# Shifted due times, corrected planned durations and a second row buffer in a planned attention-plus-experts kernel

## The chip, the cores and the metric

The kernel runs on one core of one Trainium2 chip. The metric is the device time of one execution in microseconds (us), the median of several runs. A difference under 0.3% can't be told from no change here.

## The reference, cut to what matters

Three layers follow each other. Linear attention gives 2304 tokens of 512 values; a gated layer maps each token 512 to 1536 to 512; and a router sends each token to one of 8 experts, each 512 to 1024 to 512.

```python
def phi(x):                                  # attention, 32 heads of 576 x 64, 128 features
    h = einsum('bhsd,md->bhsm', x, omega) - sum(x * x) / 2
    return exp(h - max(h)) / sqrt(m)
kv, z = einsum('bhsm,bhsd->bhmd', phi(k), v), sum(phi(k), axis=2)
x = einsum('bhsm,bhmd->bhsd', phi(q), kv) / (einsum('bhsm,bhm->bhs', phi(q), z) + 1e-6)
xn = x / sqrt(mean(x * x) + 1e-6) * rms_g    # gated layer, 2304 x 512
x = silu(xn @ w_gate) * (xn @ w_val) @ w_out
logits = x @ w_gate2 + modality_bias[modality_id]
e = argmax(logits); gate = softmax(logits)[e]
out = gate * (maximum(x @ w1[e], 0) @ w2[e]) # each token by its own expert
```

## The kernel before, in words

The program is not written in the order in which it runs. The code calls `plan.op(engine, cost, want, fn, ...)` for some 3100 pieces of work, each one or a few instructions, and names the buffers that each reads and writes. `Plan.run` then plays the pieces through with the planned durations (`cost`) and fixed delays between engines (`LAG`). At each moment an engine that is free takes, among the pieces whose inputs are there and whose buffers have room, the one with the lowest due time `want`. A piece with several possible engines goes to the first that is free. What comes out is one fixed list of instructions for each engine, and each engine works its list strictly in order, waiting where an input isn't there. So a due time or a planned duration changes no instruction's work: it changes its place in a list, and for pieces with a choice the engine.

The work in order of time: attention features of 18 tiles of 128 tokens (project L511 to L513, minimum L521, exponentials L527, transposes L542), sums over k (L576) and products with them (L727), normalization and RMS scaling (L778 to L791, on GpSimd or VectorE). Two tiles make a chunk; `enter` transposes its tokens (L1015), `hidden` multiplies them with the gate and value weights (L1036, two pieces of 12 matmuls per block of 128 columns, 12 blocks), `project` multiplies with the output weights (L1094). There are 9 chunks. Numbers are carried in two parts, a rounded one and a remainder; the remainder is a subtraction by the helper at L287, on VectorE or GpSimd.

The weights of the gated layer come in as 64-bit floats and are converted on VectorE (L844, L851, L859), then scaled and split. The experts' weights are scaled, split and written back to DRAM (`matrix`, L937 to L994) meanwhile.

`result` takes a finished chunk's two tiles: transposes (L1133), router products (L1160), scores (L1180 to L1185), and writes the rows to DRAM. Its row buffer `r` comes from the area `x2T`, which holds one tile. After the last two tiles the slots of the experts are found on VectorE (`late_values` L1594, `experts` L1635, `late_indices` L1671). A slot is 128 tokens of one expert. Three early slots, all of one expert, are worked while the routing goes on. Then 17 late slots follow: `fetch` reads the slot's expert number and loads its weights in four parts of 1 MB (L1708, on SyncE) into a ring of three places, GpSimd gathers the tokens (L1748), PE transposes them (L1737) and works up pieces (L1771, 24 matmuls of 128 columns) and down pieces (L1800, 6 matmuls of 512 columns), four of each per slot. Up to 8 more slots stand behind branches on the number of slots in use (`rest_plan`).

```python
key = len(o.costs) > 1 and e == "dve" and not o.phase, o.want, o.n
if (best is None or key < least) and all(b.at or self.free(b) for b in o.takes):
    best, least = o, key
```

Of the kernel before, what the change touches and what calls it, by code (L numbers as in the profile page):

```python
# [9 lines left out]
F32 = mybir.dt.float32  # L10
# [12 lines left out]
P = 128  # L23
# [17 lines left out]


class Buf:

# [18 lines left out]
class Plan:  # L63
# [6 lines left out]
    def __init__(self, view, banks):  # L70
        self.ops, self.view, self.banks, self.live = [], view, banks, {}
        self.phase, self.users, self.before = 0, {}, {}

    def op(self, eng, cost, want, fn, reads=(), writes=(), fills=(), after=(), lag=None, holds=()):
# [72 lines left out]
    def run(self):  # L147
# [4 lines left out]
        def enter(o):  # L152
            for e in o.costs:
                idle[e].append(o)
            heapq.heappush(events, (o.ready, o.n, None))

        for o in self.ops:
            if not o.missing:
                enter(o)
# [52 lines left out]
def kernel(  # L212
# [14 lines left out]
    nc = tc.nc  # L227
# [6 lines left out]
    KD = DM // P  # L234
# [102 lines left out]
    for j in range(2):  # L337
        area("x01", (f"xh{j}", 2048, 1), (f"xl{j}", 2048, 1))
    areas["x2s"], areas["x2T"] = areas["raw"], areas["v1"]
    area("xs", ("xh", 1024, 2), ("xl", 1024, 2))  # L340
    area("om", ("om", 1024, 2))
# [132 lines left out]
    def features(u, want, banks, q_bank):  # L474
# [73 lines left out]
        if i < EXACT:  # L548
# [9 lines left out]
        plan.op(  # L558
            "dve", 0.6, want,
            lambda: nc.vector.scalar_tensor_tensor(  # L560
# [267 lines left out]
    def block(f):  # L828
# [3 lines left out]
        for t in range(3):  # L832
# [9 lines left out]
        plan.op(  # L842
            "dve", 1.3, want,
            lambda: nc.vector.tensor_scalar(  # L844
# [156 lines left out]
    class Chunk:  # L1001
# [5 lines left out]
        def enter(self, j, want, after=()):  # L1007

            x = x_t.pop(2 * self.c + j)
            pt = buf("t", [P, KD, P], F32)  # L1010

            def transposes():
                xf = x.tile.rearrange("p h d -> p (h d)")
                for kk in range(KD):
                    nc.tensor.transpose(pt[:, kk, :], xf[:, kk * P : (kk + 1) * P], ident)  # L1015

            r = slice(j * P, (j + 1) * P)
            h, lo = self.x
            plan.op("pe", 0.43, want, transposes, reads=[x], writes=[pt], holds=self.x, after=after)
            plan.op(  # L1020
                "act", 0.48, want, lambda: nc.scalar.copy(h[:, :, r], pt.tile),
                reads=[pt], fills=[h],
            )
            plan.op(
                "dve", 0.6, want, lambda: rest(nc.vector, lo[:, :, r], pt.tile, h[:, :, r]),
                reads=[pt, h], fills=[lo],
            )
# [80 lines left out]
        def result(self, j, want, out_want):  # L1108
# [3 lines left out]
            plan.op(  # L1112
                {"act": 0.5, "dve": 0.6}, None, want,
                lambda e: copy_on(e, x2[:, :DM], self.acc[j].tile, 2.0),
# [3 lines left out]
            s2 = buf("s2", [P, 3], F32)  # L1118
            r = buf("x2T", [P, KD, P], F32)
            plan.op(  # L1120
# [10 lines left out]
            def transposes():  # L1131
# [14 lines left out]
            plan.op(  # L1146
                "dve", 0.6, out_want, lambda: rest(nc.vector, r.tile, pt.tile, top.tile),
                reads=[pt, top], writes=[r],
# [539 lines left out]
    def slots(plan, which, start, main):  # L1688
# [9 lines left out]
        def load(s, want):  # L1698
# [4 lines left out]
            def fetch(c, w):  # L1703
                if c == 0:
                    src_e = e0_i[0:1, 0:1] if s == 0 else slot_i[0:1, s : s + 1]
                    regs["e"] = nc.values_load(src_e, engines=(SP,), min_val=0, max_val=E - 1)
                src = split_dram[bass.ds(regs["e"], 1), c].rearrange("a p n -> p (a n)")
                nc.sync.dma_start(out=w.tile, in_=src)  # L1708
# [143 lines left out]
    while s < NSLOT:  # L1852
        group = range(s, min(s + (1 if s == NFIXED else 2), NSLOT))
        with tc.If(n_slots > s):
            rest_plan = Plan(view, banks)
            rest_plan.phase = 1
            for b in (idx, slot_i, sc_s, split_b, *x2_b):
                b.writers, b.readers = [], []
            slots(rest_plan, group, 0, False)
            rest_plan.run()  # L1860
# [71 lines left out]
```

## Time and profile before

| | us |
|---|---|
| runs, median (all) | 886.61 (884.8, 886.61, 887.37) |
| the profiled execution | 884.56 |
| its span, first to last instruction | 882.8 |
| PE busy | 832.1 |
| VectorE busy | 556.4 |
| ScalarE busy | 472.3 |
| GpSimd busy | 298.3 |

PE is TensorE's matmuls, PEld its weight loads, DVE VectorE, ACT ScalarE, POOL GpSimd, SP SyncE. A line number names a line of the kernel before, printed above. PEclk is the granted clock of TensorE as a share of 2.4 GHz; 0.5 is the lower level, 1.2 GHz. A busy share is a mean over stages with different limits, so the stages are to be read one by one.

### The profile page before, as it was taken

The numbers are of one execution on the slowest core, as the hardware profiler recorded it, in microseconds if no ns is written. First come the engines' busy times: TensorE is split into PE (matmuls) and PEld (weight loads), VectorE is DVE, ScalarE is ACT, GpSimd is POOL, SyncE is SP. The second block draws the span as 40 slices with busy tenths as digits, with TensorE's granted clock in tenths as the row PEclk, the third lists the DMA queues.
The fourth block names the chain that finished last, engine by engine and source line by source line (L and its number), as shares of the span: only waits on it lengthen the run. The fifth ranks groups of instructions, "written<-read, shape, count | busy, mean of one in ns | idle before, by whom it ended". The sixth has DMA issues, their size and how long they took to land. (4 is left out here: it accounts for less than half of the span.)

```text
span 882.8 us, 19258 instructions
## 1 busy us (share of the span) xinstructions
PE 832.1 (94%) x7482; PEld 690.6 (78%) x7482; DVE 556.4 (63%) x1284; ACT 472.3 (53%) x1114; POOL 298.3 (34%) x400
## 2 busy tenths in 40 slices
PE   7889999889999999999899999999997999999991
PEld 6778878678988888888788888888874777777770
DVE  6999699867768879868877979726472121121210
ACT  4764454476767778777767768432322333332230
POOL 0383468624324433424423423312312122122110
PEclk9979999899999999999999999999998999999997
DMA  8624353315376565574556664203319999999960
GB/s 289 220 102 175 120 185 126 144 60 169 119 251 216 185 226 201 171 294 156 198 191 215 223 237 181 108 1 149 104 50 384 424 425 424 424 424 424 425 280 12
DMA packets 39157, 192.29 MB, mean 218 GB/s; under 512 B 5135, under 2 KB 5263, under 8 KB 21648
## 3 DMA queue, kind: packets, MB, share of 16 engines
q1 hardware_dynamic: 35856, 180.92, 54.3%
q0 software_dynamic: 3200, 10.01, 2.9%
q8 instruction: 66, 1.08, 0.5%
q14 instruction: 35, 0.29, 0.1%
HBM read 147.88 MB, written 43.55 MB: 217 GB/s over the span
## 5 line engine op out<-in xcount | busy, mean ns | idle before, releaser
L1036 PE MATMUL bank<-x,big 128*128 128x256 f16 x2592 | 307.4, 273 | 3.8 <-DVE plain L1069 3.8
L1036 PEld LDWEIGHTS <-big 128*128 128x128 f16 x2592 | 246.8, 99 | 45.8 <-issue 17.5
L1094 PE MATMUL bank<-wo,hs 128*128 128x512 f32 x648 | 179.9, 414 | 1.2 <-POOL hs L287 1.2
L1094 PEld LDWEIGHTS bank<-wo,hs 128*128 128x128 f32 x648 | 116.4, 193 | 22.8 <-POOL hs L287 2.4
L287 POOL TENSOR_TENSOR hs<-plain,hs 128x256 fp32r<-128x256 f32 x92 | 76.9, 837 | 153.2 <-ACT hs L277 98.5
L1771 PEld LDWEIGHTS <-big 128*128 128x128 f16 x1920 | 112.3, 98 | 16.4 <-DMA big<-split_dram 1.6
L1771 PE MATMUL bank<-plain,big 128*128 128x128 f16 x1920 | 117.8, 219 | 2.6 <-DMA big<-split_dram 1.4
L1800 PE MATMUL bank<-big,plain 128*128 128x512 f16 x480 | 116.8, 382 | 0.7 <-DVE plain L287 0.7
L287 DVE TENSOR_TENSOR plain<-plain 128x512 f16<-128x512 f32 (+1 forms) x44 | 31.6, 720 | 127.5 <-ACT plain L277 127.3
L812 DVE SCALAR_TENSOR_TENSOR big<-big,e_fac 128x512 f16<-128x512 f32 x128 | 107.2, 860 | 6.2 <-ACT big L818 6.0
L1054 ACT ACTIVATE plain<-bank,w_scale 128x256 f32<-128x256 f32 x108 | 51.3, 475 | 84.6 <-PE bank L1036 65.4
L527 ACT ACTIVATE plain<-bank,plain 128x128 f32<-128x128 f32 x256 | 72.7, 370 | 24.7 <-DVE plain L521 21.4
L946 ACT ACTIVATE plain<-big,plain 128x1024 bf16<-128x1024 f32 x64 | 73.5, 1149 | 9.7 <-DMA big<-in_w_exp_dram 9.5
L1800 PEld LDWEIGHTS <-plain 128*128 128x128 f16 x480 | 44.6, 98 | 41.7 <-DVE plain L287 1.5
L818 ACT ACTIVATE big<-big,e_fac 128x512 f16<-128x512 f32 x103 | 72.0, 722 | 1.2 <-DMA split_dram<-big 1.2
L1061 DVE SCALAR_TENSOR_TENSOR plain<-plain,bank 128x256 f32<-128x256 f32 x108 | 44.4, 413 | 33.4 <-ACT plain L1054 33.0
L287 POOL TENSOR_TENSOR xs<-plain,xs 128x256 fp32r<-128x256 f32 x45 | 38.6, 860 | 71.3 <-ACT xs L277 55.6
L1788 ACT ACTIVATE plain<-bank 128x512 f32<-128x512 f32 x40 | 23.9, 598 | 68.8 <-PE bank L1771 68.5
L521 DVE TENSOR_REDUCE plain<-bank 128x4 f32<-128x512 f32 x66 | 45.1, 683 | 16.7 <-PE bank L513 12.4
L1069 DVE SCALAR_TENSOR_TENSOR plain<-bank,w_scale,plain 128x256 f32<-128x256 f32 x108 | 51.1, 477 | 0.6
L277 ACT CAST hs<-plain 128x256 fp32r<-128x256 f32 x84 | 33.8, 405 | 30.8 <-DVE plain L1069 21.7
L1815 POOL TENSOR_TENSOR plain<-plain,x 128x1 f32<-128x1 f32 x17 | 3.9, 231 | 130.7 <-ACT plain L818 100.8
(252 smaller groups left out, 1186.2 us busy)
## 6 DMA issues: line engine op xcount, KB each, us to landing
big<-split_dram SPq DMA_DIRECT2D x72, 1024.0 KB, 21.6
big<-in_w_exp_dram SPq DMA_DIRECT2D x32, 1024.0 KB, 6.8
split_dram<-big SPq DMA_DIRECT2D x32, 1024.0 KB, 8.6
big<-in_w_moe_dram SPq DMA_DIRECT2D x36, 512.0 KB, 4.5
plain<-in_v_dram SPq DMA_DIRECT2D x18, 260.0 KB, 3.9
x_dram<-plain SPq DMA_DIRECT2D x18, 258.0 KB, 3.5
plain<-in_kT_dram SPq DMA_DIRECT2D x16, 256.0 KB, 2.9
plain<-in_qT_dram SPq DMA_DIRECT2D x16, 256.0 KB, 2.7
```

The lines of the kernel that those rows point to most:

```text
L287: eng.tensor_tensor(out=out, in0=src, in1=hi, op=ALU.subtract)
L521: lambda: nc.vector.tensor_reduce(out=mx.tile, in_=pp.tile, axis=AX.X, op=ALU.min),
L527: nc.scalar.activation(ph[:, h, :], pp[:, h, :], AF.Exp, bias=mx[:, h : h + 1], scale=-1.0)
L812: nc.vector.scalar_tensor_tensor(out=out, in0=src, scalar=factor, in1=hi, op0=ALU.mult, op1=ALU.subtract)
L818: nc.scalar.activation(out, src, AF.Copy, scale=factor)
L946: lambda c=c, h=h, cs=cs: nc.scalar.activation(junk.tile, raws[c][:, cs], AF.Square, bias=tiny, accum_out=sums[:, 2 * c + h : 2 * c + h + ...
L1036: nc.tensor.matmul(gv[:, t, :], w[a][:, kk, :], self.x[x][:, kk, :], start=kk == 0 and m == 0, stop=kk == KD - 1 and m == 2,)
L1054: lambda: nc.scalar.activation(th.tile, gv[:, 0, :], AF.Tanh, scale=w_scale[:, f, 2:3]),
L1069: lambda: nc.vector.scalar_tensor_tensor(out=th.tile, in0=gv[:, 1, :], scalar=w_scale[:, f, 4:5], in1=th.tile, op0=ALU.mult, op1=ALU.mult,),
L1094: nc.tensor.matmul(self.acc[j].tile, a[:, r], w_in(f, i, 2), start=f == 0 and m == 0, stop=f == FT - 1 and m == 2,)
L1771: nc.tensor.matmul(ph[:, j, :], w_of(c, p, k * F2 + (4 * n + j) * P, P), x[a][:, kk, :], start=kk == 0 and j == 0 and m == 0, stop=kk == K ...
L1800: nc.tensor.matmul(y.tile, hs[n][a][:, kk, :], w_of(2 + n, p, kk * DM, DM), start=f == 0 and m == 0, stop=f == KF2 - 1 and m == 2,)
```

## The change

A table `NUDGES` shifts the due times of 32 runs of pieces, by their number in the order of the calls, by -6 to +6; a due time of 12 more is one chunk, or one slot, later. The shifts are applied in `Plan.run` of the main plan alone, not in those behind the branches. Planned durations of some pieces on VectorE and ScalarE are set anew (0.6 to 0.68 or 0.69, 0.48 to 0.58, 0.5 to 0.6, 1.3 to 1.05). The last chunk's two tiles take their row buffer from an area of two places. Since a shift moves the third part of one slot's weights ahead of its first, `fetch` reads the expert number with whichever part comes first. No instruction is added or taken away in what is computed. Of the table one line and its end are shown.

```diff
--- before.py
+++ after.py
@@ -40,6 +40,18 @@
 EXPERTS_FROM, EXPERTS_TO = 25.0, 85.0
 
 
+
+NUDGES = (
+    (214, 214, 0.5), (257, 257, -2), (270, 270, 4), (288, 293, 1), (305, 311, -0.5),
...
+    (2549, 2549, -4), (3005, 3005, -2),
+)
+
+
 class Buf:
 
 
@@ -70,6 +82,7 @@
     def __init__(self, view, banks):
         self.ops, self.view, self.banks, self.live = [], view, banks, {}
         self.phase, self.users, self.before = 0, {}, {}
+        self.nudged = True
 
     def op(self, eng, cost, want, fn, reads=(), writes=(), fills=(), after=(), lag=None, holds=()):
 
@@ -154,6 +167,9 @@
                 idle[e].append(o)
             heapq.heappush(events, (o.ready, o.n, None))
 
+        for first, last, shift in NUDGES if self.nudged else ():
+            for o in self.ops[first : last + 1]:
+                o.want += shift
         for o in self.ops:
             if not o.missing:
                 enter(o)
@@ -337,6 +353,7 @@
     for j in range(2):
         area("x01", (f"xh{j}", 2048, 1), (f"xl{j}", 2048, 1))
     areas["x2s"], areas["x2T"] = areas["raw"], areas["v1"]
+    areas["x2E"] = areas["v1"] + areas["v0"]
     area("xs", ("xh", 1024, 2), ("xl", 1024, 2))
     area("om", ("om", 1024, 2))
     area("hs", ("hh", 1024, 2), ("hl", 1024, 2))
@@ -556,7 +573,7 @@
             reads=[pt], writes=[ft],
         )
         plan.op(
-            "dve", 0.6, want,
+            "dve", 0.68, want,
             lambda: nc.vector.scalar_tensor_tensor(
                 out=ft[:, 1], in0=pt.tile, scalar=PSC, in1=ft[:, 0],
                 op0=ALU.mult, op1=ALU.subtract,
@@ -840,7 +857,7 @@
             )
         lo32, hi32 = (lambda: raw[:, :, :, 0]), (lambda: raw[:, :, :, 1])
         plan.op(
-            "dve", 1.3, want,
+            "dve", 1.05, want,
             lambda: nc.vector.tensor_scalar(
                 bits.tile, hi32(), 3, 0x3FFFFFFF, ALU.logical_shift_left, ALU.bitwise_and
             ),
@@ -1018,11 +1035,11 @@
             h, lo = self.x
             plan.op("pe", 0.43, want, transposes, reads=[x], writes=[pt], holds=self.x, after=after)
             plan.op(
-                "act", 0.48, want, lambda: nc.scalar.copy(h[:, :, r], pt.tile),
+                "act", 0.58, want, lambda: nc.scalar.copy(h[:, :, r], pt.tile),
                 reads=[pt], fills=[h],
             )
             plan.op(
-                "dve", 0.6, want, lambda: rest(nc.vector, lo[:, :, r], pt.tile, h[:, :, r]),
+                "dve", 0.69, want, lambda: rest(nc.vector, lo[:, :, r], pt.tile, h[:, :, r]),
                 reads=[pt, h], fills=[lo],
             )
 
@@ -1110,13 +1127,13 @@
             i = 2 * self.c + j
             x2 = buf("x2s", [P, XC], F32)
             plan.op(
-                {"act": 0.5, "dve": 0.6}, None, want,
+                {"act": 0.6, "dve": 0.69}, None, want,
                 lambda e: copy_on(e, x2[:, :DM], self.acc[j].tile, 2.0),
                 reads=[self.acc[j]], writes=[x2],
             )
 
             s2 = buf("s2", [P, 3], F32)
-            r = buf("x2T", [P, KD, P], F32)
+            r = buf("x2E" if self.c == NCH - 1 else "x2T", [P, KD, P], F32)
             plan.op(
                 "act", 0.82, out_want,
                 lambda: nc.scalar.activation(
@@ -1144,7 +1161,7 @@
                 reads=[pt], writes=[top],
             )
             plan.op(
-                "dve", 0.6, out_want, lambda: rest(nc.vector, r.tile, pt.tile, top.tile),
+                "dve", 0.69, out_want, lambda: rest(nc.vector, r.tile, pt.tile, top.tile),
                 reads=[pt, top], writes=[r],
             )
             plan.op(
@@ -1701,7 +1718,7 @@
             regs = {}
 
             def fetch(c, w):
-                if c == 0:
+                if not regs:
                     src_e = e0_i[0:1, 0:1] if s == 0 else slot_i[0:1, s : s + 1]
                     regs["e"] = nc.values_load(src_e, engines=(SP,), min_val=0, max_val=E - 1)
                 src = split_dram[bass.ds(regs["e"], 1), c].rearrange("a p n -> p (a n)")
@@ -1853,7 +1870,7 @@
         group = range(s, min(s + (1 if s == NFIXED else 2), NSLOT))
         with tc.If(n_slots > s):
             rest_plan = Plan(view, banks)
-            rest_plan.phase = 1
+            rest_plan.phase, rest_plan.nudged = 1, False
             for b in (idx, slot_i, sc_s, split_b, *x2_b):
                 b.writers, b.readers = [], []
             slots(rest_plan, group, 0, False)
```

The first 52 pieces of PE keep their order; from there on the lists of all engines differ. Pieces with a choice of engine change it too: 33 pass from VectorE or ScalarE to GpSimd and 29 leave it. Three places follow. Lines of the changed kernel are 16 or 17 higher than those of the kernel before.

GpSimd, near 60 us, before: L779 to L791 is the RMS scaling of one tile (twice here), L287 a remainder, `xs` an attention input.

```order
L790 TENSOR_SCALAR plain<-plain 128x512
L791 TENSOR_TENSOR plain<-plain 128x512
L287 TENSOR_TENSOR xs<-plain,xs 128x256
L779 TENSOR_SCALAR plain<-plain 128x1
L780 TENSOR_TENSOR plain<-plain 128x1
L790 TENSOR_SCALAR plain<-plain 128x512
L791 TENSOR_TENSOR plain<-plain 128x512
L287 TENSOR_TENSOR wo<-big,wo 128x512
```

The same place of the changed kernel (L796 to L808 the scaling, L303 a remainder):

```order
L807 TENSOR_SCALAR plain<-plain 128x512
L808 TENSOR_TENSOR plain<-plain 128x512
L303 TENSOR_TENSOR xs<-plain,xs 128x256
L796 TENSOR_SCALAR plain<-plain 128x1
L797 TENSOR_TENSOR plain<-plain 128x1
L303 TENSOR_TENSOR xs<-plain,xs 128x256
L807 TENSOR_SCALAR plain<-plain 128x512
L808 TENSOR_TENSOR plain<-plain 128x512
L303 TENSOR_TENSOR wo<-big,wo 128x512
```

A second remainder of an attention input (`xs`) stands between the two halves of the second tile's scaling.

PE, near 435 us, before: L1160 is the end of a tile's router products, L1015 the transposes of a tile that enters a chunk, L1094 a projection; `bank_90` and the like are PSUM banks.

```order
L1160 MATMUL bank_90<-route_w,plain 128x16
L1160 LDWEIGHTS plain
L1160 MATMUL bank_90<-route_w,plain 128x8
L1015 MATMUL bank_90<-ident,plain 128x128 x4
L1094 MATMUL bank_93<-wo,hs 128x512 x3
L1094 MATMUL bank_94<-wo,hs 128x512 x3
```

The same transposes in the changed kernel (L1032; L744 products with the sums over k, L1111 a projection, L1053 gate or value products):

```order
L744 LDWEIGHTS plain
L744 MATMUL bank_91<-plain 64x65
L1111 MATMUL bank_93<-wo,hs 128x512 x3
L1111 MATMUL bank_94<-wo,hs 128x512 x3
L1032 MATMUL bank_92<-ident,plain 128x128 x4
L1053 LDWEIGHTS big
L1053 MATMUL bank_90<-x_393,big 128x256
```

The router products no longer stand ahead of the transposes, which write another bank than before.

VectorE, at the end of the routing, before: L1599 to L1606 end `late_values`, L1635 to L1644 begin `experts`.

```order
L1599 TENSOR_TENSOR x_393<-x_393,xs 128x504
L1605 TENSOR_SCALAR x_393<-x_393,xs 128x18x28
L1606 TENSOR_TENSOR x_393<-x_393,xs 128x18x28
L1635 TENSOR_SCALAR x_393<-x_393 128x1
L1636 TENSOR_SCALAR x_393<-xs,x_393 128x28
L1637 TENSOR_TENSOR x_393<-x_393 128x224
L1644 TENSOR_REDUCE x_393<-x_393 128x28
```

And in the changed kernel:

```order
L1616 TENSOR_TENSOR x_393<-x_393,xs 128x504
L1622 TENSOR_SCALAR x_393<-x_393,xs 128x18x28
L1623 TENSOR_TENSOR x_393<-x_393,xs 128x18x28
L303 TENSOR_TENSOR plain<-plain 128x512
L1652 TENSOR_SCALAR x_393<-x_393 128x1
L1653 TENSOR_SCALAR x_393<-xs,x_393 128x28
L1654 TENSOR_TENSOR x_393<-x_393 128x224
```

A remainder of an early slot's rows (L303) now stands between the two.

## Rows read from the trace of the kernel before

**Rows 1.** The page: busy time and share, then what the DMA queues moved by slice
```profile
PE 832.1 (94%) x7482; PEld 690.6 (78%) x7482; DVE 556.4 (63%) x1284; ACT 472.3 (53%) x1114; POOL 298.3 (34%) x400
...
GB/s 289 220 102 175 120 185 126 144 60 169 119 251 216 185 226 201 171 294 156 198 191 215 223 237 181 108 1 149 104 50 384 424 425 424 424 424 424 425 280 12
```

**Rows 2.** Windows by stage: length, busy (count) of PE, PEld, DVE, ACT, POOL; PEclk, DMA, GB/s
```profile
0.00:44.00 44.00, 36.79 (x232) 32.73 (x232) 34.43 (x72) 27.70 (x90) 9.41 (x19) 1.00 0.74 256
44.00:210.00 166.00, 154.12 (x1169) 132.01 (x1170) 142.45 (x252) 91.45 (x233) 93.49 (x106) 0.93 0.35 123
210.00:640.00 430.00, 425.11 (x3685) 368.23 (x3684) 323.70 (x837) 283.93 (x675) 152.18 (x219) 1.00 0.52 184
640.00:677.00 37.00, 29.99 (x304) 20.04 (x303) 20.20 (x74) 9.21 (x19) 5.65 (x8) 0.91 0.45 180
677.00:865.00 188.00, 186.14 (x2101) 137.62 (x2098) 35.61 (x53) 59.48 (x98) 36.55 (x47) 1.00 0.95 397
```

**Rows 3.** Windows, same columns: the stretches at the lower clock up to 640 us
```profile
43.70:53.90 10.20, 8.91 (x41) 8.51 (x42) 8.97 (x14) 4.65 (x11) 8.96 (x9) 0.50 0.07 27
64.20:67.60 3.40, 3.40 (x11) 2.11 (x9) 3.40 (x5) 2.87 (x9) 3.22 (x6) 0.50 0.76 251
166.60:173.40 6.80, 5.88 (x17) 4.40 (x16) 6.20 (x10) 3.85 (x11) 4.50 (x8) 0.50 0.66 254
197.30:200.70 3.40, 3.40 (x17) 2.67 (x17) 2.73 (x5) 0.38 (x1) 3.32 (x4) 0.50 0.00 0
436.20:439.70 3.50, 3.50 (x30) 2.51 (x29) 3.18 (x10) 2.63 (x9) 0.78 (x1) 0.51 0.89 227
```

**Rows 4.** Waits of PE: total us, times, longest us
```profile
PE bank L727 <- ACT plain L277: 2.9, 1, 2.9
...
PE bank L1015 <- POOL plain L791: 1.5, 1, 1.5
```

**Rows 5.** Timeline of POOL near 60 us: start, duration, engine, line, operation
```profile
61.12 1.26 POOL L791 TENSOR_TENSOR plain<-plain 128x512 f32<-128x512 f32 x1
```

**Rows 6.** Line L287 on POOL, input remainders: ns min/median/max, first and last start
```profile
L287 POOL TENSOR_TENSOR xs<-plain,xs x45: 717/732/2310, 45.9 to 525.8; 128x256 fp32r<-128x256 f32 x45
```

**Rows 7.** Timeline of DVE and PE, 432 to 436 us; idle before and releaser in brackets
```profile
432.61 0.44 PE L1160 MATMUL bank<-route_w,plain 128*128 128x24 bf16 x12
...
435.23 0.17 DVE L1180 TENSOR_REDUCE logits<-bank 128x8 f32<-128x24 f32 x1
...
435.55 0.63 PE L1015 MATMUL bank<-ident,plain 128*128 128x128 f32 x4 [2.49 <-DVE logits L1180]
```

**Rows 8.** Timeline of PE, 648 to 677 us
```profile
649.45 0.45 PE L1160 MATMUL bank<-route_w,plain 128*128 128x24 bf16 x12
...
652.78 0.17 PE L1447 MATMUL bank<-xs 128*128 128x8 bf16 x1
...
671.61 1.11 PE L1737 MATMUL bank<-ident,plain 128*128 128x128 f32 x4 [5.32 <-DMA plain<-x_dram,x]
...
676.85 0.33 PE L1771 MATMUL bank<-plain,big 128*128 128x128 f16 x3
```

**Rows 9.** Timeline of SyncE: the first loads of the late experts' weights
```profile
662.13 4.88 SPq L1708 DMA_DIRECT2D big<-split_dram  x8
```

**Rows 10.** Line L1708, the load issued at 792.0 us, and its landing
```profile
L1708 SPq DMA_DIRECT2D big<-split_dram x1: 333/333/333, 792.0 to 792.0; - x1
...
DMA to landing us min/median/max: 22.2/22.2/22.2
```

**Rows 11.** Line L1708, the load issued at 827.5 us, and its landing
```profile
L1708 SPq DMA_DIRECT2D big<-split_dram x1: 337/337/337, 827.5 to 827.5; - x1
...
DMA to landing us min/median/max: 19.2/19.2/19.2
```

**Rows 12.** Timeline of PE near 814 us
```profile
814.25 2.85 PE L1771 MATMUL bank<-plain,big 128*128 128x128 f16 x48 [1.45 <-DMA big<-split_dram]
```

**Rows 13.** Timeline of PE, its last products
```profile
859.37 5.34 PE L1800 MATMUL bank<-big,plain 128*128 128x512 f16 x24
```

5 rows, old and new, of the table NUDGES are left out of this document.

## The prediction

> **What bounds the kernel now.** I read the page first: TensorE is busy 832.1 of 882.8 us [rows 1], so what a change of order can give is its idle time and the work that it does at half clock. The windows by stage say where these lie [rows 2]. PE is idle for 44.0 - 36.8 = 7.2 us in the first 44 us, 166.0 - 154.1 = 11.9 from 44 to 210, 4.9 in the long stretch to 640, 7.0 in the routing (640 to 677) and 1.9 in the late experts; then 17.8 us of ending follow in which PE does nothing. DVE is busy 142 of 166 us between 44 and 210: there the weights of the gated layer are converted beside the attention, and PE waits for it and for POOL.
>
> Idle time costs twice where the granted clock falls. Rows 3 show five stretches at half of full clock (1.2 in place of 2.4 GHz) before 640 us. A piece of matmuls there takes about twice as long, so half of PE's busy time in them is lost: 8.9 / 2 = 4.5, then 1.7, 2.9, 1.7 and 1.75 us. The first begins within the longest wait before them [rows 4], the last with the wait of 2.5 us at 435 us [rows 7].
>
> The last 190 us have another limit. From 677 to 865 us the DMA engines are 95% busy, and their rate stays at 424 to 425 GB/s over seven slices of the page and 384 in the first [rows 1, 2]. The loads of the late experts' weights start at 662.1 us, when SyncE can read the experts' numbers [rows 9]. The part issued at 792.0 takes 22.2 us and lands at 814.2 [rows 10], and PE, after 1.45 us of waiting for it, begins at 814.25 [rows 12]. So PE's work before 814 doesn't set the end. Call S the time of the first load. The end of PE is S + (814.25 - 662.13 = 152.1) + the work that remains after that part, 50.5 us (PE's last products end at 859.37 + 5.34 = 864.7 [rows 13]): S + 202.6. What counts is when S comes and how much work stands behind each part.
>
> **The change part by part.** It adds and removes no computation, so I sum waits.
>
> First 44 us, and the wait of 2.9 us after it: PE's first 52 pieces keep their order, and ACT and DVE keep theirs in what feeds them, but for one 0.4 us piece on DVE. I take 0, and the 4.5 us of slow clock stay too.
>
> 44 to 210 us, the rest: 11.9 - 2.95 = 8.9 us of waits and 1.7 + 2.9 + 1.7 = 6.3 us of clock, 15.3 together. The new lists move the weights' pieces ahead of attention pieces by up to ten places on DVE, and attention pieces back by 10 to 20 places on PE. In the second half of this stretch a piece of attention and its successor stood four to nine pieces apart and now mostly seven to eleven, so that more work covers the same chain. Against it stands one place that gets worse. Near 60 us PE waited 1.5 us for the second half of an RMS scaling on POOL [rows 4], which starts its last instruction at 61.12 [rows 5]. Now a remainder of an input stands ahead of it, 0.73 us by the median and 2.31 at most [rows 6]; the wait becomes 2.2 to 3.8 us. Whether the rest closes half or all of its gaps no row shows. By the rows the ends are a gain of 15.3 and, if as many new waits open as old ones close and that one grows, a loss of 2.3. I take a gain of 6, somewhat under the middle, since ten waits are moved and some will reappear.
>
> The Trainium skill, "SBUF — State Buffer", section "Who interferes with whom", says that GpSimd and VectorE share one port pair, that a two-input VectorE instruction contends with GpSimd's reads, and that the one that comes first holds the pair. The spread from 717 to 2310 ns for one form [rows 6] agrees. By that rule the inserted remainder, which runs beside VectorE's weight pieces, costs the upper end, 2.3 us, where the median would say 0.7.
>
> 210 to 640 us: 4.9 us of waits and 1.75 of clock. At 435 us the transposes of a tile wait for the scores that read the same PSUM bank: the router products begin at 432.6, the first reading of the bank only at 435.2, behind other work on DVE, and PE stands for 2.49 us [rows 7]. The new order has the router products behind the transposes and another bank under these. 2.5 + 1.75 = 4.2 us go. What is late next there is the gate product behind it, which needs only DVE's usual pieces. The other 2.4 us are four short waits; I keep them and add 0.7 for new ones: a gain of 3.5. Ends: 6.6 gained, 2 lost (the same wait somewhere else).
>
> Routing, to S: ahead of the last router products [rows 8] two up pieces of 1.34 us now stand behind and one token transposition of 0.44 ahead: 2.2 us earlier. Three up pieces (4.0 us) stand between them and the rank products in place of 652.78 - 649.45 = 3.3: 0.7 later, and one remainder of 0.69 is put before the expert numbers on DVE: together 1.4 later. S comes 0.8 earlier. The second row buffer frees the last tile's square on ACT, but its transposes still stand behind the other tile's router products on PE, so I count it as nothing; at most it gives the 0.7 us of that square.
>
> The wait of 5.3 us for the gathered tokens at 671.6 [rows 8] shrinks, since two down pieces now go ahead of those transposes. I count nothing: the late experts follow the loads, and PE would only wait later.
>
> Late experts: behind the part that bound at 814 three pieces fewer remain. The new limit is the first part of the last slot. It is issued at 827.5 and lands 19.2 us later, at 846.7 [rows 11], or S + 184.6. In the new list 13 pieces follow from its first use, where 9 did, each 5.34 / 4 = 1.335 us [rows 13]: S + 201.9, against S + 202.6. A gain of 0.7. The moved load of one part delays two others of that slot by one part each; by the same count they end near S + 201, below that limit.
>
> Sum: 6 + 3.5 + 0.8 + 0.7 = 11.0 us. From the profiled execution's 884.56 (span 882.8 and 1.8 around it) this gives 873.6. The median of the runs is 2.05 higher, so I forecast 886.6 - 11.0 = 875.6 us.
>
> **The rivals.**
> - *The gaps only move.* The planner's fixed delays don't know a POOL instruction of 0.7 or 2.3 us [rows 6], so new waits open where it sees none. For it: 33 pieces go to POOL. Against: the 435 us place, where the cause itself is gone. Stage gains fall to 1 or 2 us: 885, within 0.3%.
> - *The place near 60 us turns the sign.* If the grown wait reaches 3.8 us, PE is at half clock again for as long as after the first wait, 10.2 us, where it was 3.4 [rows 3]: 2.3 for the wait and (10.2 - 3.4) / 2 = 3.4 for the clock, 5.7 us. Nothing behind takes it up, since S follows PE. It decides from the point where the remainder runs at 2.3 us; if the other gains before 640 us fail as well, only routing and late experts are left against it: 5.7 - 1.5 = 4.2 us slower, 890.8.
> - *All gaps close.* 15.3 + 6.6 + 1.5 = 23.4 us: 863.
> - *PE bounds the late experts after all.* If the loads run faster once they start, the 5.3 us at 671, and 1.7 for two short waits and as much for the clock before it, come off the end too: 6 to 8 us more, 868. Against: the flat 424 GB/s [rows 1]. The Trainium skill, "DMA: Bandwidth & Descriptors", section "Where 436 GB/s comes from", gives 435 GB/s as the ceiling, 2.5% above the trace; by an estimate from it 192 us of loads could shrink by 5 us at most.
>
> **How the numbers follow.** Chances: my forecast (869 to 882) 0.44, gaps only move 0.18, the sign turns 0.14, all gaps close 0.12, PE bounds the late experts 0.12. A difference under 0.3% (2.7 us) can't be told from none. Faster: 0.44 + 0.12 + 0.12 and a small part of the second case, 0.70. Same: 0.16. Slower: 0.14. The likeliest case's own range is 869 to 882; the one for 8 in 10 reaches over the gaps that only move and to the fuller gains: 863 to 888.
>
> **What would show it.** Right: a PE wait of about 2.9 us near 45 us as before; no wait of over 1 us at the transposes near 430 us; PE idle from 44 to 210 down to 6 us or so, with fewer stretches at 0.5; the first late load near 650 us; 201 to 203 us from it to PE's last product, with waits for the weights spread over the late slots in place of the one at the gather. Wrong: an interval from first load to end that is shorter than 198 us (then PE bounded that stage), a first load later than 662 us (then the gaps only moved), or a wait of over 3 us near 62 us with a long stretch at half clock.

## The result, and the profile after

The changed kernel takes 877.91 us (median of 4 runs, 875.57 to 879.51); the kernel before 886.12 (4 runs). The ratio is 0.991, 95% interval 0.989 to 0.9929: 8.2 us less, where 11.0 were forecast. The profiled execution of the changed kernel took 879.51, the highest of its four, and that of before 884.56, under its median; between these two traces there are 5.05 us.

The page of the changed kernel, the rows that answer to [rows 1]:

```profile
PE 830.9 (95%) x7482; PEld 691.3 (79%) x7482; DVE 564.5 (64%) x1286; ACT 467.3 (53%) x1108; POOL 307.7 (35%) x404
...
GB/s 291 221 118 160 193 103 127 156 61 113 194 248 217 217 210 209 198 239 131 208 237 154 219 220 203 145 19 227 22 118 416 426 425 424 424 425 424 424 177 24
```

The windows by stage, with the columns of [rows 2], and the stretches at half clock up to 640 us, as in [rows 3]:

```profile
0.00:44.00 44.00, 37.19 (x232) 33.01 (x232) 34.40 (x72) 27.99 (x90) 8.08 (x19) 1.00 0.74 256
44.00:210.00 166.00, 155.17 (x1191) 134.11 (x1192) 141.27 (x248) 94.34 (x245) 102.42 (x114) 0.95 0.35 123
210.00:640.00 430.00, 429.55 (x3782) 371.06 (x3780) 338.75 (x863) 280.85 (x671) 155.30 (x219) 1.00 0.53 185
640.00:677.00 37.00, 26.27 (x287) 19.64 (x285) 16.91 (x57) 7.24 (x13) 6.61 (x9) 0.89 0.70 280
677.00:865.00 188.00, 182.75 (x1999) 133.46 (x1997) 33.16 (x48) 56.91 (x93) 35.33 (x45) 0.98 0.90 377
...
44.20:54.40 10.20, 9.32 (x43) 8.92 (x44) 8.66 (x14) 4.96 (x15) 9.44 (x10) 0.50 0.09 27
64.70:68.10 3.40, 3.40 (x18) 3.40 (x17) 2.14 (x3) 1.30 (x3) 2.74 (x5) 0.50 0.36 133
177.30:180.70 3.40, 3.25 (x16) 2.26 (x16) 1.95 (x5) 3.16 (x8) 2.14 (x3) 0.50 0.79 270
```

PE's idle time is 6.8 us in the first stage, where it was 7.2; 10.8 from 44 to 210 in place of 11.9; and 0.45 in the long stretch in place of 4.9. No stretch at half clock is left between 210 and 640 us. The loads of the late experts' weights start at 651.66 us (SyncE's timeline), where they started at 662.13 [rows 9]:

```profile
651.66 21.96 SPq L1725 DMA_DIRECT2D big<-split_dram  x14
```

That is 10.5 us earlier. But PE ends 4.7 us earlier only. Its timeline after the routing and its last products, beside [rows 8, 13]:

```profile
650.22 6.63 PE L1817 MATMUL bank<-big,plain 128*128 128x512 f16 x30
661.88 1.03 PE L1754 MATMUL bank<-ident,plain 128*128 128x128 f32 x4 [5.03 <-DMA plain<-x_dram,x]
665.81 1.12 PE L1754 MATMUL bank<-ident,plain 128*128 128x128 f32 x4 [2.90 <-DMA plain<-x_dram,x]
666.72 6.54 PE L1788 MATMUL bank<-plain,big 128*128 128x128 f16 x96
673.10 0.61 PE L1754 MATMUL bank<-ident,plain 128*128 128x128 f32 x4
676.51 1.09 PE L1754 MATMUL bank<-ident,plain 128*128 128x128 f32 x4 [2.81 <-DMA plain<-x_dram,x]
...
854.70 5.34 PE L1817 MATMUL bank<-big,plain 128*128 128x512 f16 x24
```

Three waits for gathered tokens, 10.7 us together, stand where one of 5.3 stood. From the first load to PE's end it is now 854.70 + 5.34 - 651.66 = 208.4 us; before it was 202.6. No wait for weights is left: the part that the prediction named as the new limit, the first of the last slot, is issued at 822.5 and lands 13.8 us later, at 836.3 or S + 184.6, the prediction's own figure. PE first uses it at 842.8, 6.5 us later. This is its line, as in [rows 11]:

```profile
L1725 SPq DMA_DIRECT2D big<-split_dram x1: 342/342/342, 822.5 to 822.5; - x1
...
DMA to landing us min/median/max: 13.8/13.8/13.8
```

### The profile page after: what moved, and what is told of

Same layout as the page of the kernel before. It is cut to its first block, busy times and chain, and to the rows that moved or that the text cites. A ratio compares the mean times of both kernels' runs of the same rounds, so it can differ in the third digit from the quotient of the medians.

```text
span 877.6 us, 19233 instructions
## 1 busy us (share of the span) xinstructions
PE 830.9 (95%) x7482; PEld 691.3 (79%) x7482; DVE 564.5 (64%) x1286; ACT 467.3 (53%) x1108; POOL 307.7 (35%) x404
## 5 line engine op out<-in xcount | busy, mean ns | idle before, releaser
L1053 PE MATMUL bank<-x,big 128*128 128x256 f16 x2592 | 309.3, 274 | 5.2 <-DVE plain L1086 4.7
L1053 PEld LDWEIGHTS <-big 128*128 128x128 f16 x2592 | 246.8, 99 | 48.0 <-issue 19.2
L1111 PE MATMUL bank<-wo,hs 128*128 128x512 f32 x648 | 177.5, 407 | 0.0
L303 POOL TENSOR_TENSOR hs<-plain,hs 128x256 fp32r<-128x256 f32 x95 | 81.3, 857 | 138.8 <-ACT hs L293 88.9
L1111 PEld LDWEIGHTS bank<-wo,hs 128*128 128x128 f32 x648 | 113.0, 189 | 19.3 <-POOL hs L303 0.7
L1788 PE MATMUL bank<-plain,big 128*128 128x128 f16 x1920 | 120.5, 221 | 0.0
L303 DVE TENSOR_TENSOR plain<-plain 128x512 f16<-128x512 f32 (+2 forms) x48 | 34.0, 710 | 125.3 <-ACT plain L293 125.2
L835 ACT ACTIVATE big<-big,e_fac 128x512 f16<-128x512 f32 x95 | 67.2, 723 | 0.9 <-DMA split_dram<-big 0.8
L303 POOL TENSOR_TENSOR xs<-plain,xs 128x256 fp32r<-128x256 f32 x47 | 39.2, 834 | 63.3 <-ACT xs L293 47.2
L538 DVE TENSOR_REDUCE plain<-bank 128x4 f32<-128x512 f32 x66 | 45.2, 685 | 16.1 <-PE bank L530 11.9
```

The costliest lines, as they stand in the source:

```text
L303: eng.tensor_tensor(out=out, in0=src, in1=hi, op=ALU.subtract)
L538: lambda: nc.vector.tensor_reduce(out=mx.tile, in_=pp.tile, axis=AX.X, op=ALU.min),
L835: nc.scalar.activation(out, src, AF.Copy, scale=factor)
L1053: nc.tensor.matmul(gv[:, t, :], w[a][:, kk, :], self.x[x][:, kk, :], start=kk == 0 and m == 0, stop=kk == KD - 1 and m == 2,)
L1111: nc.tensor.matmul(self.acc[j].tile, a[:, r], w_in(f, i, 2), start=f == 0 and m == 0, stop=f == FT - 1 and m == 2,)
L1788: nc.tensor.matmul(ph[:, j, :], w_of(c, p, k * F2 + (4 * n + j) * P, P), x[a][:, kk, :], start=kk == 0 and j == 0 and m == 0, stop=kk == K ...
```

## The experiments

Twelve kernels were run, each timed beside the kernel before on the same chip; ratios are to that kernel, with their 95% intervals. In `swap240`, `act44` and `tuned` the lists come out of the planner as in the changed kernel, and then a few pieces are moved by hand, so that nothing else differs.

**What the parts of the change are worth.**

`costs_only`, without the table:

```diff
-NUDGES = ( ... 32 entries ... )
+NUDGES = ()
```

> The changed kernel without the table of shifts (corrected durations and the second row buffer stay). Theory 'the durations do it': the planner sees ScalarE's and VectorE's pieces at their real length, so the gaps close by themselves: 877 to 879, as with the whole change. Theory 'the shifts do it': durations alone only move the gaps, 884 to 887; the wait near 435 us is then likely back in another place. Both parts needed: 880 to 884. The remainder on GpSimd ahead of the RMS scaling near 60 us stands here too, so the wait of 3.5 us there should be seen in this run by either theory.

892.59 us, 1.0066 (1.0047 to 1.0084): slower than before, against all three forecasts. The corrected durations make other lists, and these have a wait of 4.7 us of their own in the long stretch (PE's timeline), which moves the routing back: S is 669.1.

```profile
416.96 1.44 PE L1053 MATMUL bank<-x,big 128*128 128x256 f16 x6 [4.71 <-DVE plain L1086]
```

PE's wait near 60 us is 3.6 us here as in the whole change, and the remainder stands ahead of the scaling in GpSimd's list; with the shifts alone (`nudges_only`, next) the wait is 1.5 us and no remainder stands there. So this comes from the durations, not from the shifts.

`nudges_only`, the table with the old durations (`0.68` back to `0.6`, `1.05` to `1.3` and so on) and one row buffer:

> The changed kernel with the old durations and one row buffer for the last two tiles; the table of shifts stays. Theory 'the shifts do it': 877 to 880. Theory 'the shifts were found for these durations': with the old ones the lists come out differently, the shifts land on other neighbours, and the time is 884 to 890, no better than before. By the second theory the sum of this gain and that of the durations alone is well under the whole 8 us.

879.59 us, 0.9913 (0.9894 to 0.9931). The shifts with the old durations give a gain that can't be told from that of the whole change; the second theory falls. Yet they don't simply add up with the durations: -0.87% and +0.66% would make -0.2%, and the whole change has -0.9%.

`n_first` and `n_second`, the changed kernel with the shifts before piece 900, and with those from it on:

```diff
-NUDGES = ( ... 32 entries ... )
+NUDGES = ( ... the first 12, up to (859, 865, 0.5) ... )     # n_first
+NUDGES = ( ... the last 20, from (971, 971, -4) ... )        # n_second
```

> The changed kernel with only the shifts that begin before piece 900 (12 of 32; they work before 220 us). All shifts gave 877.9, none 892.6, the later twenty alone 894.5. If the early shifts carry the gain by themselves: 878 to 881. If either half is worth little without the other (the later ones were found on the lists that the early ones leave): 884 to 890, with the waits of 1 to 5 us in the long stretch still there.

> The changed kernel with only those shifts that begin at piece 900 or later (20 of 32; they work from about 232 us on). If the shifts gain mostly at the long stretch and the routing: 881 to 884, against 892.6 without any shift. If the first twelve, which work before 220 us, carry the gain: 889 to 892.

`n_first` takes 885.29, 0.9984 (0.9965 to 1.0003); `n_second` 894.45, 1.0088 (1.0062 to 1.0114). By themselves the later twenty gain nothing (1.0088 against 1.0066 with none); behind the first twelve they are worth 0.7% (0.991 against 0.9984). So a shift here has no price of its own. It works only on the lists that the earlier ones leave.

`no_x2E`, one row buffer for the last two tiles:

```diff
-r = buf("x2E" if self.c == NCH - 1 else "x2T", [P, KD, P], F32)
+r = buf("x2T", [P, KD, P], F32)
```

> The changed kernel with the row buffer of one place for the last two tiles as before. The lists differ from the changed kernel's only from the routing on. The prediction's step (the second buffer is worth nothing, at most 0.7 us): 877 to 879, S within 1 us of 651.7. Rival: the buffer is what brings the last tile's routing forward, S comes 2 us or more later and the time is 880 or more.

876.90 us, 0.9921 (0.9893 to 0.9949), S at 652.0. The second buffer is worth nothing that can be told from noise, as the prediction's step had it.

**The place near 60 us.** `swap240`:

```diff
+        if self.nudged:
+            order.remove(self.ops[240])
+            order.insert(order.index(self.ops[144]) + 1, self.ops[240])
```

> The changed kernel with one remainder of an attention input put behind the RMS scaling near 60 us on GpSimd, where it stood before the change; all else in the lists is the same. In the changed kernel PE waits 3.6 us for that scaling, before it was 1.5. Theory 'the remainder costs what the wait grew by': 2 us less, 875 to 876.5, with the wait back at 1.5 us. Rival 'the wait grew because the scaling itself ran slower (2.26 in place of 0.69 us for its first half) beside VectorE': the wait falls by 0.7 only and the time stays, 877 to 878. Rival 'something behind takes it up': the wait falls but PE arrives at the routing at the same time: 877.5 to 878.5.

879.03 us, 0.9917 (0.9891 to 0.9943). In the changed kernel PE waits 3.56 us here, and its GpSimd timeline shows why: the remainder took its usual 0.72 us, but the first half of the scaling behind it 2.26.

```profile
60.06 0.72 POOL L303 TENSOR_TENSOR xs<-plain,xs 128x256 fp32r<-128x256 f32 x1
60.77 2.26 POOL L807 TENSOR_SCALAR plain<-plain 128x512 f32<-128x512 f32 x1
63.11 1.31 POOL L808 TENSOR_TENSOR plain<-plain 128x512 f32<-128x512 f32 x1
```

VectorE, in the same kernel at that time, runs a two-input instruction on the weights from 60.80 to 62.55:

```profile
60.80 1.75 DVE L876 SCALAR_TENSOR_TENSOR big<-big 128x1536 uint32<-128x1536 uint32 x1
```

In `swap240` the remainder is out of the way, and the next instruction on GpSimd is the one that meets it (the same VectorE instruction stands there from 59.60 to 61.35):

```profile
59.00 0.69 POOL L810 TENSOR_SCALAR plain<-plain 128x512 f32<-128x512 f32 x1
59.78 2.70 POOL L811 TENSOR_TENSOR plain<-plain 128x512 f32<-128x512 f32 x1
```

PE's wait is 2.87 us, 0.7 less, and not 1.5: on the wait the first rival holds. (The time, 879.03, can't be told from the changed kernel's, so it does not choose between the rivals.) The rest of the growth came from the moment at which the scaling meets VectorE. In both kernels the slow instruction ends about as long after VectorE's as it takes alone (62.55 + 0.69 = 63.24, measured 63.03; 61.35 + 1.26 = 62.61, measured 62.48). That is what the Trainium skill, "SBUF — State Buffer", section "Who interferes with whom", says of the shared port pair: the one that comes second is blocked, not slowed. Which one came second is plain in `swap240` alone (VectorE at 59.60, GpSimd at 59.78); in the changed kernel GpSimd's record starts 0.03 us ahead of VectorE's, and yet it was GpSimd that waited. The prediction had used this rule for the remainder itself, which was not the one that was hit.

**What bounds the late experts.** `lag7`, a longer planned delay between a late gather and its transposes:

```diff
-writes=[xg], lag=3.0,
+writes=[xg], lag=3.0 if early else 7.0,
```

> The changed kernel with one number changed: the planner's delay behind a late slot's gather is 7.0 in place of 3.0 us, so that from the end of the routing on PE has one slot's transposes ahead of the first late up pieces in place of two, and one fewer behind them. In the changed kernel PE waits there 5.0, 2.9 and 2.8 us for gathered tokens. Theory A (PE bounds the late experts after the change, the weights land 6.5 us or more ahead of their use): the waits of 2.9 and 2.8 us and one stretch at half clock go, 871 to 874. Theory B, the prediction's (the late experts follow the loads, so a wait for the gathered tokens costs nothing): 877 to 879, and new waits for weights of 5 us or so in the late slots.

878.78 us, 0.9913 (0.9892 to 0.9934): no gain, and no wait for weights either, so neither theory as written. In its PE timeline the second slot's transposes no longer wait, but they had covered the time in which the first slot's tokens are copied and split, and PE now waits for that instead:

```profile
661.89 0.90 PE L1754 MATMUL bank<-ident,plain 128*128 128x128 f32 x4 [4.96 <-DMA plain<-x_dram,x]
664.88 0.37 PE L1788 MATMUL bank<-plain,big 128*128 128x128 f16 x2 [2.08 <-ACT plain L293]
...
675.04 0.66 PE L1754 MATMUL bank<-ident,plain 128*128 128x128 f32 x4 [1.99 <-DMA plain<-x_dram,x]
```

10.7 us of waits, all for tokens, became 9.0: 7.0 for tokens and 2.1 for the copy.

`xg4_lag7`, four places for gathered tokens besides:

```diff
-areas["xg"] = [ ... for k in range(2)]
+areas["xg"] = [ ... for k in range(2)] + areas["seed"] + areas["v0"]
```

> The changed kernel with the delay of 7.0 us behind late gathers, and four places in place of two for the gathered tokens, so that the third and fourth gather needn't wait for PE's transposes of the first. Theory A (PE is late by its waits for gathered tokens, the loads have room): the wait of 2.0 us for the third slot's tokens goes and the sum of these waits falls from 9.0 in the kernel with the delay alone to 7 us or less; 875 to 877. Rival (gathers at the same time slow each other and the loads): the first gather lands later, no gain: 878 to 880.

878.10 us, 0.9896 (0.987 to 0.9922). The waits fall to 3.9 + 2.2 + 0.9 = 7.0 us (the 2.2 for the copy), as theory A has it, and a wait of 1.0 us for weights is back at 776.8. The time lies in the rival's range, though the first gather did not land later, and can't be told from the changed kernel's.

`gather_first`, the loads behind the first gather (the new piece moves the numbers behind it by one, and the table's last entry, 3005, with them):

```diff
+            if s == NEARLY:                     # in compute, behind the gather
+                gate = plan.op("dma", 0.1, want - 30,
+                    lambda: nc.sync.dma_start(out=gate_dram, in_=xg.tile[0:1, 0:4]), reads=[xg])
+                late_loads.append(gate)
...
+        for gate in late_loads:                 # every load of a late slot waits for it
+            for o in held:
+                o.missing += 1
+                gate.users.append(o)
```

> The changed kernel, but SyncE's loads of the late experts' weights wait until the first late slot's gathered tokens have landed (a small copy of these tokens, queued ahead of the loads). In the changed kernel the gathers land 8.4 and 9.8 us after their issue, beside loads at 420 GB/s; the early gathers, without such loads, took 3.5. Theory A (the loads beside them slow the gathers): the first gather lands within 5 us, the PE waits for gathered tokens fall from 10.7 to 4 us or less. Rival: the gather's 8 us are its own: nothing shortens. For the time: if the late experts follow the loads with a floor of S + 202.6 us (before 202.6; S is the first load), S comes near 658 and the end at 860: 877 to 879, no gain. If PE alone bounds and the loads have 6.5 us to spare, the shorter waits come through: 871 to 874.

On the gathers theory A is shown. The gathers' line in this kernel, first those issued at 655.7 and 658.3, ahead of the loads (the landing of one is recorded), then the two issued at 662.4 and 663.7, beside them (408 GB/s from 662.4 to 673.1):

```profile
L1765 POOL DMA_INDIRECT plain<-x_dram,x x2: 971/979/987, 655.7 to 658.3; - x2
...
DMA to landing us min/median/max: 3.3/3.3/3.3
...
L1765 POOL DMA_INDIRECT plain<-x_dram,x x2: 950/967/984, 662.4 to 663.7; - x2
...
DMA to landing us min/median/max: 8.8/9.1/9.4
```

In the changed kernel the four late gathers took 7.5 to 9.7 us. The time answers neither forecast: 890.23 us, 1.004 (1.0022 to 1.0057). S came only at 660.4, since the copy itself had to be issued (659.1) and the expert number read behind it. PE waited 3.3 us for the first weights; and the planner, which counts 4.3 us for a gather, put two later transposes too close behind theirs (waits of 4.9 us at 693.7 and 4.8 at 812.2). From S to the end it is 211.5 us.

`before_lag7`, the same delay in the kernel before:

> The kernel before with one number changed, the planner's delay behind a late slot's gather, 7.0 in place of 3.0: two more down pieces (2.7 us) stand ahead of the first late transposes. The prediction's reading of the kernel before (the late experts follow the loads, S + 202.6): the PE wait of 5.3 us for the gathered tokens falls to about 2.7, waits for weights near 814 us grow by as much, S + 202 to 203 stays, 885 to 888, no change. Rival, PE bounds there: 2.5 to 4 us come off, 882 to 884.

883.98 us, 0.9977 (0.9963 to 0.9991). The wait for gathered tokens falls by 1.65 us, from 5.32 to 3.67, and S to end is 202.1 in place of 202.6: in the profile most of that wait is hidden, as the prediction read it. But the waits for weights did not grow by as much; 0.8 us of them remain where there were 1.45. The median, 2 us lower, lies in the rival's range, but 0.23% is less than what can be told from no change, so it is not shown whether PE's waits cost something even before.

The profiles of all kernels, put side by side (S is the first late load, the end is PE's last product; the last column is PE's waits for gathered tokens after S):

| kernel | S | end | S to end | token waits |
|---|---|---|---|---|
| n_second | 671.7 | 874.2 | 202.5 | 3.7 |
| costs_only | 669.1 | 872.0 | 202.9 | 5.0 |
| n_first | 663.7 | 868.0 | 204.3 | 5.1 |
| before | 662.1 | 864.7 | 202.6 | 5.3 |
| before_lag7 | 661.3 | 863.4 | 202.1 | 3.7 |
| gather_first | 660.4 | 871.9 | 211.5 | 11.6 |
| nudges_only | 658.5 | 861.1 | 202.6 | 5.2 |
| xg4_lag7 | 655.4 | 859.9 | 204.5 | 4.8 |
| act44 | 655.1 | 862.1 | 207.0 | 10.2 |
| tuned | 653.1 | 861.8 | 208.7 | 10.9 |
| no_x2E | 652.0 | 856.2 | 204.1 | 7.6 |
| lag7 | 651.8 | 857.9 | 206.2 | 7.0 |
| **after** | 651.7 | 860.1 | 208.4 | 10.7 |
| swap240 | 649.9 | 853.8 | 203.9 | 8.5 |

Each row is one execution. No kernel goes below 202.1. Of the seven with S at 658 or later five lie between 202.1 and 202.9; four of these still wait 0.4 to 1.45 us for weights, so the loads set the pace (`n_second` has no such wait; `n_first`, at 204.3, waits 2.1 us for weights at 816; `gather_first` is told above). The seven with an earlier S lie 1.8 to 6.6 us above 202.1, and all but `xg4_lag7` wait nowhere for weights (over 0.2 us): there PE's own chain sets it.

The earlier S need not be the cause. The same seven share an order of PE's list: five down pieces in a row ahead of the first late transposes, and later two or more slots' transposes back to back, behind the first late slot's up pieces. `before`, `nudges_only`, `n_first`, `costs_only` and `n_second` have a down piece between one slot's transposes and the next. No run has the early S with that order, so the table doesn't tell the two apart.

**Two versions meant to be faster.** `act44` moves the square of one tile (L791) on ScalarE behind the two copies that PE waits for at 44.9 us. `tuned` does that, gives the RMS scaling near 60 us to VectorE, and puts the first scatter behind the second gather:

```diff
+        if self.nudged:
+            self.ops[144].eng = "dve"                                        # tuned alone
+            for n, behind in ((101, 118), (100, 118), (144, 126), (2681, 2732)):   # act44: the first two
+                order.remove(self.ops[n])
+                order.insert(order.index(self.ops[behind]) + 1, self.ops[n])
```

> The changed kernel with only the square on ScalarE near 44 us behind the two copies. The wait there is the same in the kernels before and after (2.95 and 2.97 us), and a stretch of 10.2 us at half clock follows it in both. Theory A: the wait falls to 1.2 us and the stretch at half clock gets shorter or goes: 2 to 6 us less than the changed kernel, 872 to 876. Rival (the clock falls there whatever PE waited): 1.8 us less at most, 876 to 877. Rival (something behind takes the gain up): 877.5 to 878.5.

> The changed kernel with three places of its lists set by hand, all else word for word the same: the square of one tile on ScalarE near 44 us goes behind the two copies that PE waits for; the RMS scaling near 60 us is done by VectorE in place of GpSimd; the first scatter of results after the routing goes behind the second gather on GpSimd. Theory A (what PE gains early comes out at the end, while S + 202.6 isn't reached): the wait at 44.9 us falls from 3.0 to 1.2, that at 64.5 from 3.6 to 0.5, the second gather's from 2.9 to 1.6; 6 us and what the clock gives back: 870 to 873. Rival (the weights' loads are the floor: S comes earlier by the early gains, so the floor moves with them; only the gather's part is lost): 872 to 875. Rival (VectorE, loaded there with the weights, passes the 0.8 us on and PE waits for it): 876 to 878.

`act44` takes 880.04, 0.9933 (0.9904 to 0.9961); `tuned` 880.92, 0.9937 (0.9913 to 0.9961). Neither beats the changed kernel, and both lie above all their ranges. In `act44` the wait falls from 2.97 to 1.74 us, now for VectorE, but the square that comes later brings its tile's scaling later, and PE waits for that six microseconds on (its timeline), where it had waited 0.21:

```profile
44.90 1.42 PE L748 MATMUL bank<-plain 128*128 128x65 f32 x8 [1.74 <-DVE plain L775]
...
50.70 1.11 PE L1036 MATMUL bank<-ident,plain 128*128 128x128 f32 x4 [1.82 <-POOL plain L812]
```

The half clock did not go with the first wait. It lasts 13.7 us in this execution, 45.5 to 59.2 (windows, the columns of before):

```profile
45.50:59.20 13.70, 11.88 (x58) 10.84 (x58) 11.81 (x21) 5.02 (x14) 11.12 (x12) 0.50 0.08 20
```

In `tuned` the wait near 60 us falls from 3.56 to 1.52, but the half clock at 45.7 lasts 13.7 us as well, the second gather's wait falls by 1.2 us, and the fourth's grows from 2.8 to 5.0. The time stays.

## Why the prediction was right, and where it was not

The sum was right in direction and near in size: 8.2 us by the medians for 11.0, 877.9 in the range of the likeliest case. Its steps were not equally right, and part of the agreement is luck: two errors before the routing cancelled, and the loss behind it was smaller in the median than in the profile.

- *First 44 us and the wait after it, 0.* Right: 2.97 us in place of 2.95, and 10.2 us of half clock in both.
- *44 to 210, a gain of 6.* Too high. Idle time fell by 1.05 us. PE's work at half clock fell from 3.4 + 5.88 + 3.4 to 3.40 + 3.25 us, and half of the difference is 3.0; the longer first stretch takes 0.2 back. That is 3.8 together. The place near 60 us cost 2.1, as the ends of 2.2 to 3.8 for its wait allowed; and one new wait of 2.8 at 177.5 came for two of 1.2 and one of 2.1 that went. The rival that the clock there would be lost for 10.2 us did not come: it is 3.4 us as before.
- *210 to 640, a gain of 3.5.* Too low: 4.4 us of idle time and 1.75 of clock, 6.2, close to the upper end. The cause at 435 us was named rightly: the transposes no longer stand behind the scores (they run at 426.8 us and wait for nothing), and no wait over 0.5 us is left. That the other four short waits would stay was wrong.
- *Routing, S earlier by 0.8.* The three terms to S make 10.3 us, and S came 10.5 earlier; by the stages 0.4 + 3.8 + 6.2 = 10.4 of that is before 640, so the routing itself gave about nothing. The errors of the stages cancelled. The second row buffer is worth nothing that can be told (`no_x2E`).
- *Late experts, S + 201.9, a gain of 0.7; the gather's wait counts nothing.* This step failed: -5.8 us in the profiled execution, 208.4 in place of 201.9. The limit by the loads is there as forecast (the last slot's first part lands at S + 184.6, and 202.1 is the lowest of 14 profiles). But in the kernel before, PE's own chain ended only 1.45 us ahead of the loads (its one wait for weights, [rows 12]), and in the changed kernel it is the later one. The windows from S to the end give the size: PE idle 208.4 - 197.4 = 11.0 us against 202.6 - 195.0 = 7.6, so 3.5 more; and busy 2.3 more, with two stretches at half clock after 660 in place of one.

Where in the stage this lies, the first late up pieces show. They begin at S + 15.1 (666.72), before at S + 14.7 (676.85, [rows 8]): up to there PE followed S to within 0.3 us. The first wait for tokens was to shrink and did so by 0.3 us only; the second, of 2.90, stands where before there was a down piece of 2.77 (at 672.52). Behind this point both profiles have 2101 matmuls, and these take 193.3 us in place of 187.9, with 1.5 us more idle and 3.9 more busy. The windows from S to the end after, from the first late up pieces after and before, then the stretches at half clock after and before:

```profile
651.66:860.05 208.39, 197.36 (x2133) 144.33 (x2130) 40.01 (x63) 60.29 (x99) 40.69 (x52) 0.97 0.93 386
666.72:860.05 193.33, 190.22 (x2101) 140.72 (x2099) 36.26 (x53) 59.09 (x97) 35.34 (x45) 0.98 0.93 388
...
676.85:864.71 187.86, 186.29 (x2101) 137.76 (x2099) 35.76 (x53) 59.27 (x97) 36.55 (x47) 1.00 0.95 398
...
662.00:668.80 6.80, 3.90 (x28) 3.44 (x29) 2.08 (x3) 1.27 (x2) 3.28 (x5) 0.50 1.02 426
675.70:682.50 6.80, 5.99 (x34) 4.30 (x35) 0.00 (x0) 0.00 (x0) 0.00 (x0) 0.50 1.01 429
...
668.30:675.10 6.80, 3.49 (x11) 1.85 (x12) 0.69 (x1) 0.59 (x1) 1.15 (x2) 0.50 1.02 420
```

So the loss is the wait of 2.81 us for the fourth slot's tokens at 676.51, which stands where before there was the one of 1.45 for weights, and work at half clock behind the waits: before, the stretch ends ahead of the up pieces; now the first reaches 2 us into them and the second lies wholly behind. The fourth gather could start only at 667.7, behind PE's transposes of the second slot, and landed 8.7 us after its start, where the planner counts 4.3.

The prediction looked at this rival only from the side of faster loads ("PE bounds the late experts after all"), where it would have been a gain. The wait for the gathered tokens was in its list, and was costed at nothing because the cover, the late loads, was taken as given; it did not ask how thin that cover was, though it had the 1.45 us. The term is off by 6.5 us in this execution. `swap240`, with the same lists from the routing on, came through the stage in 203.9 us, 2.4 us of the difference in idle time and 2.1 in busy time, and `no_x2E` in 204.1. So this part varies from one execution to the next, which fits the medians' difference of 8.2 us against 5.05 in the two traces.

Of its signs, three came: 2.97 us near 45 us, no wait at the transposes near 430 us, the first late load at 651.7. Two did not: PE's idle time from 44 to 210 is 10.8 us and not 6, and from S to the end it is 208.4 us with no wait for weights. Of the signs of being wrong, a wait over 3 us near 62 us came, but with a short stretch at half clock.

What is open: what the waits and the half clock behind them are each worth in the median. `xg4_lag7` took 3.7 us of waits out, its interval is 3.9 shorter, and its median is the same as the changed kernel's; its S was 3.7 later in that execution. Open too is whether PE's order or the earlier S made PE's chain the later one (the table above).

## What to carry to other kernels

When a stage has a floor that starts with an event, work out both chains from that event, the transfer's and the engine's, and the distance between them. Here it was 1.45 us: an engine's wait is free only within it, and a change that also reorders the engine's list behind the event can use it up. And where a planner writes the order, a shift or a corrected duration has no price of its own: the same twenty shifts were worth nothing alone and 0.7% behind twelve others, and truer durations alone made the kernel slower, so judge such edits only on the lists that they leave.

## What was not expected of the hardware

- A gather of 128 rows landed in 3.3 us with no other loads under way and in 8.8 to 9.4 beside loads at 408 GB/s, within one execution of `gather_first`.
- Executions of one kernel lie up to 9 us apart (`swap240`: 873.30 to 882.38), and profiles of kernels with the same lists up to the routing show the early half clock at other places: from 44.2 us for 10.2 in the changed kernel, from 28.0 for 3.4, 45.1 for 6.8 and 62.2 for 10.2 in `no_x2E`, though PE's waits there are the same to 0.8 us. A gain of 2 us at one wait is hard to see over that in six runs: the intervals here are 0.2 to 0.3% to either side.
